# Chunked scan with a two-layer MLP: the first sweep's second matmul in plain fp32, decay masks moved ahead of the sums, and partial sums added by accumulating transfers

## The chip, the cores and the metric

The kernel runs on one core of a Trainium2 chip. TensorE (PE), VectorE (DVE), ScalarE (ACT), GpSimd (POOL) and SyncE (SP, which issues the transfers) each work through their own list of instructions in order, and wait for one another by semaphores. The metric is the device time of one execution in microseconds, the median over runs.

## The reference

Four batches of eight heads are scanned in chunks; the result, transposed to 3072 tokens of 256 values, goes through a two-layer MLP.

```python
cum = np.cumsum(log_a_chunk, axis=-1)
L = np.exp(cum[:, :, :, None] - cum[:, :, None, :]) * causal
M = np.einsum('bhin,bhjn->bhij', Cc, Bc) * L
y = np.einsum('bhij,bhjd->bhid', M, xc)
y += np.einsum('bhin,bhnd->bhid', Cc, state) * np.exp(cum)[:, :, :, None]
state = decay_full * state + np.sum(Bx, axis=2)

h = x @ w_in              # x: 3072 x 256, w_in: 256 x 2048
g = h - np.tanh(h)
out = g @ w_out           # w_out: 2048 x 256
```

The weights arrive as float64, all else is float32.

## The kernel before

**The scan.** The kernel cuts each batch of 768 positions into seven chunks of up to 112 (`Q`), 28 in all. A chunk needs the matrix `lt` (the decays, exponentials of differences of running sums, times C·B, zero above the diagonal), then `chunk_y` multiplies it by `x` on PE. The state that a chunk hands on stands in 16 extra rows of the next chunk's `x`, copied there by ACT (`copies`, L566), so that the chunks are a chain. The output of a chunk is split into two fp32r numbers, `xh` (ACT) and `xl` (DVE), so that two or three fast fp32r products give nearly a full fp32 product.

Chunks 0 to 2, which the first tile of tokens needs, get `lt` in `first_tile`: for each half of the heads, `fn_f` sums the logs `la` on PE into `cp`, `fn_x` takes four exponentials on ACT with a bias `ncum` for each head (L404), `fn_m` multiplies by C·B on DVE (L409), and `fn_s` zeroes what lies above the diagonal on POOL (L414). Chunks 3 to 9 get their sums from PE instead (`chunk_a`, L451), from tiles `lt_c` and `rt_c` of sums in three bf16 parts, which are sent through DRAM (`put_parts`, `get_parts`). `rt_c` is first filled with signs by `signs` on POOL (L806). Later chunks read their sums back from DRAM (`chunk_l`).

**The weights.** A block `u` of 256 hidden columns of both weights is loaded by `load_w`, and `conv` builds floats out of the float64 bits: `fn0` on ACT (L300), `fn1` to `fn4` on DVE (L305, L310, L313, L317), `hi` on ACT (L321) and `lo` on DVE (L324). The last two leave the fp32r pair `wh`, `wl`. Block 0 is converted in two halves (w_in, then w_out), each later block whole.

**The MLP.** Tokens lie in eight tiles `t`, four of 256 and four of 512. The first four are done in four sweeps over the hidden dimension (`SWEEPS`), of two blocks `u` each, so that the weights can arrive meanwhile; the last four go over all of it at once. A step (t, f) is `mm1` (L629: 12 matmuls of 256 columns, xh·wh + xh·wl + xl·wh), `act` (tanh on ACT, L643; the subtraction on DVE, L647; the split of `g` into `gh` on ACT, L651, and `gl` on DVE, L657) and, two steps later, `mm2` (L683: 12 matmuls again, into the PSUM bank `po0`). After the first sweep `keep` copies a tile's partial sum to SBUF (`pt`, L705); after the second and third DVE adds to it (L698), and after the last DVE adds (L717) and SP stores.

**What sets the order.** Nothing is written out by hand: `Order` collects every operation with a cost and its reads and writes, and a list scheduler with a seeded jitter (`SEED`, `JITTER`, `LOOK`, `RATE`, `URGE`) writes one list for each engine. A change of a cost or of a seed so moves rows everywhere. Tiles rotate through few buffers (`ph` 2, `g` 3, `att` 1).

Of the kernel before, what the change touches and what calls it, by code (L numbers as in the profile page):

```python
# [20 lines left out]
P = 128  # L21
# [5 lines left out]
Q = P - N  # L27
# [13 lines left out]

REBIAS = 2.0 ** -112
# [6 lines left out]
APART, URGE = 5, 3.0  # L49


class Order:
# [3 lines left out]
    DMA_LATENCY, SEM, SEM_PE, RATE, FLIGHT = 0.8, 0.15, 0.28, 0.24e6, 8  # L56
    ROUNDS, JITTER, SEED, EARLY, LOOK = 16, 0.3, 69, 5.0, 0.35
# [153 lines left out]
def tile_ssm_moe(ctx: ExitStack, tc: tile.TileContext, a, x, bn, bc, wts, out):  # L211
# [76 lines left out]
    wl = cp.tile([P, NCONV, 2, 2, 256], F32R, name="wl")  # L288

    def conv(u, halves=False):  # L290
# [36 lines left out]
        for i in range(n):  # L327
# [6 lines left out]
            op("DVE", 1.2 * k, lambda s=s: fn3(s), r=[n_v[i]], w=[n_m[i]])  # L334
            op("DVE", 1.2 * k, lambda s=s: fn4(s), r=[n_m[i]], w=[n_v[i]])
# [42 lines left out]
    def first_tile():  # L378
# [32 lines left out]

        def fn_s(ck, i):
            lt = chs[ck]["l"][:, 4 * i : 4 * i + 4]
            nc.gpsimd.affine_select(out=lt, in_=lt, pattern=[[0, 4], [1, Q]], compare_op=ALU.is_ge,  # L414
                                    fill=0.0, base=N, channel_multiplier=-1)

        for ck in range(len(chunks[0])):
# [4 lines left out]
            for i in range(2):  # L422
                n_f = slot("ph", NPH)
                op("PE", 1.2, lambda ck=ck, i=i: fn_f(ck, i), r=["la", "upto"], w=[n_f])
                op("ACT", 1.05, lambda ck=ck, i=i: fn_x(ck, i), r=[n_f, "ncum", "tab"], w=[k["n_l"][i]], urge=URGE)
# [80 lines left out]
    def chunk_y(ck):  # L506
# [68 lines left out]
        def copies(n):  # L575
            return [op("ACT", 0.2, lambda i=i: fn_c(i), r=[n], w=[grp[(ck + 1) // CPG]["p_x"][(ck + 1) % CPG]], urge=first) for i in range(4)]
# [4 lines left out]
        cost = 0.72 if far else 0.62 if apart else 0.81  # L581
# [52 lines left out]

    def act(t, f):
        n_h, n_g = gs[t, f, 0]
        n_gh, n_gl = slot("gh", 3), slot("gl", 3)
        gs[t, f, 0] += [n_gh, n_gl]
# [22 lines left out]
        op("DVE", 0.69, fn_s, r=[n_h], w=[n_g])  # L661
        op("ACT", 0.62, fn_h, r=[n_g], w=[n_gh])
        op("DVE", 0.71, fn_l, r=[n_g, n_gh], w=[n_gl])

    def mm2(t, f, seg):

        w, last = WIDTH[t], f + blocks(t) == seg[1]
        _, _, n_h, n_l = gs[t, f, 0]
# [19 lines left out]
        op("PE", 12 * rate(w) * blocks(t), fn, r=[n_h, n_l, f"wh{f // 2}.1", f"wl{f // 2}.1"], w=n_po[t, seg])  # L688
# [19 lines left out]

    def store(t, seg):
        w = WIDTH[t]  # L710
        name = op.pieces(slot("ob", 2), 2)

        def fn_c(e):
            if e == 0:
                obs[t] = p2.tile([P, 2, w], F32, tag="ob", name=f"ob{t}")
            if t < NSW:
                nc.vector.tensor_tensor(out=obs[t].rearrange("p e w -> p (e w)"), in0=po[t, seg][2], in1=pts[t], op=ALU.add)  # L717
            elif e == 0:
# [7 lines left out]
        if t < NSW:  # L726
            op("DVE", 0.69, lambda: fn_c(0), r=[*n_po[t, seg], n_pt[t]], w=name)
        else:
            for e in range(2):
                op(("ACT", "DVE")[e], 0.6, lambda e=e: fn_c(e), r=[n_po[t, seg][e]], w=[name[e]])  # L730
# [13 lines left out]
    ncf = cp.tile([P, N], F32, name="ncf")  # L744
    idn = cp.tile([P, N], F32, name="idn")
# [72 lines left out]
    op("POOL", 1.6, consts_pool, w=["upto", "after", "pid"])  # L818
    op("DVE", 0.25, logs, r=["al"], w=["a"])
# [4 lines left out]
    op("ACT", 0.9, ones, w=["lt_c"])  # L824

# [68 lines left out]
    conv(1)  # L894
# [91 lines left out]
```

## Time and profile before

| | |
|---|---|
| median of 3 runs | 337.64 us (335.47 to 447.55) |
| the profiled execution, its time | 337.02 us |
| its span, first to last instruction | 335.1 us |
| what lies around the span | 1.92 us |
| PE busy | 321.2 us (96%) |
| DVE busy | 226.3 us (68%) |
| ACT busy | 218.3 us (65%) |
| POOL busy | 57.0 us (17%) |

The run of 447.55 us stands alone; the other two and the profiled execution lie within 0.7% of one another. The shares are averages over stages that differ: the scan and the first sweep take the first 62 us, and the rest is nearly all matmuls. Busy time of PE is counted to modelled ends of pipelined matmuls, so that a step's length is better read from the start of one step to the start of the next.

### The profile page before, as it was taken

The numbers are of one execution on the slowest core, as the hardware profiler recorded it, in microseconds if no ns is written. First come the engines' busy times: TensorE is split into PE (matmuls) and PEld (weight loads), VectorE is DVE, ScalarE is ACT, GpSimd is POOL, SyncE is SP. The second block draws the span as 40 slices with busy tenths as digits, with TensorE's granted clock in tenths as the row PEclk, the third lists the DMA queues.
The fourth block names the chain that finished last, engine by engine and source line by source line (L and its number), as shares of the span: only waits on it lengthen the run. The fifth ranks groups of instructions, "written<-read, shape, count | busy, mean of one in ns | idle before, by whom it ended". The sixth has DMA issues, their size and how long they took to land.

```text
span 335.1 us, 6403 instructions
## 1 busy us (share of the span) xinstructions
PE 321.2 (96%) x2452; PEld 269.7 (80%) x2452; DVE 226.3 (68%) x346; ACT 218.3 (65%) x524; POOL 57.0 (17%) x77
## 2 busy tenths in 40 slices
PE   8867989899999999999999999999999999999995
PEld 7656878899999999877877777877787778888884
DVE  5898999999888855764556656456655554545552
ACT  7868889797666635856778783676676664544441
POOL 7445463121000200301111101121011010000000
PEclk9967999999999999999999999999999999999999
DMA  7759885280000006622432033323010000100001
GB/s 219 233 183 344 234 299 161 88 298 3 0 2 2 1 33 220 209 87 86 139 121 94 32 117 99 121 94 115 13 63 2 1 0 2 63 0 2 0 0 63
DMA packets 14441, 32.16 MB, mean 96 GB/s; under 512 B 2500, under 2 KB 5452, under 8 KB 14412
## 3 DMA queue, kind: packets, MB, share of 16 engines
q1 hardware_dynamic: 14412, 31.77, 28.4%
q8 instruction: 19, 0.31, 0.4%
q14 instruction: 10, 0.08, 0.1%
HBM read 28.33 MB, written 3.43 MB: 95 GB/s over the span
## 4 chain that ended last, share of the span: by engine, by line
PE 82%; DMA 8%; DVE 4%; ACT 2%; SPq 1%; issue 1%; POOL 0%; POOLq 0%
PE o L683 39%; PE ph L629 38%; DMA raw<-w_d 5%; PE y L541 3%; PE att L528 2%; DMA bc<-bc_d 2%; DMA braw<-bn_d 1%; ACT wv L300 1%; ACT lt L404 1%; DVE gl L657 1%; ACT x L566 0%; SPq L871 0%; DVE g L647 0%; DVE wm L305 0%; DVE xl L572 0%
## 5 line engine op out<-in xcount | busy, mean ns | idle before, releaser
L647 DVE TENSOR_TENSOR g<-ph,g 128x512 f32<-128x512 f32 x96 | 66.0, 689 | 67.6 <-ACT g L643 67.4
L643 ACT ACTIVATE g<-ph 128x512 f32<-128x512 f32 x96 | 57.2, 597 | 67.6 <-PE ph L629 65.9
L629 PE MATMUL ph<-xh,wh 128*128 128x256 f32 (+1 forms) x256 | 85.8, 346 | 0.0
L629 PE MATMUL ph<-xh,wl 128*128 128x256 f32 (+1 forms) x256 | 84.6, 341 | 0.0
L657 DVE TENSOR_TENSOR gl<-g,gh 128x512 fp32r<-128x512 f32 x96 | 68.8, 716 | 20.0 <-ACT gh L651 18.9
L651 ACT CAST gh<-g 128x512 fp32r<-128x512 f32 x96 | 59.5, 620 | 26.4 <-DVE g L647 25.4
L683 PE MATMUL o<-gh,wh 128*128 128x256 f32 (+1 forms) x256 | 72.2, 343 | 0.1
L683 PE MATMUL o<-gh,wl 128*128 128x256 f32 (+1 forms) x256 | 71.2, 339 | 0.0
L683 PE MATMUL o<-gl,wh 128*128 128x256 f32 (+1 forms) x256 | 70.8, 338 | 0.0
L629 PE MATMUL ph<-xl,wh 128*128 128x256 f32 (+1 forms) x256 | 65.8, 338 | 0.2 <-DVE xl L572 0.2
L476 POOL TENSOR_SCALAR_AFFINE_SELECT lt<-lt 128x896 f32<-128x896 f32 (+1 forms) x25 | 28.0, 1121 | 202.9 <-ACT lt L494 180.4
L629 PEld LDWEIGHTS ph<-xh,wh 128*128 128x128 f32 x256 | 49.2, 192 | 7.8 <-issue 1.6
L629 PEld LDWEIGHTS ph<-xh,wl 128*128 128x128 f32 x256 | 49.2, 192 | 5.3
L629 PEld LDWEIGHTS ph<-xl,wh 128*128 128x128 f32 x256 | 44.3, 191 | 6.0 <-DVE xl L572 0.4
L683 PEld LDWEIGHTS o<-gh,wh 128*128 128x128 f32 x256 | 41.5, 188 | 7.8 <-issue 1.9
L683 PEld LDWEIGHTS o<-gl,wh 128*128 128x128 f32 x256 | 41.6, 189 | 5.5
L683 PEld LDWEIGHTS o<-gh,wl 128*128 128x128 f32 x256 | 41.4, 188 | 5.2
L494 ACT ACTIVATE lt<-lt,ncum 128x112 f32<-128x112 f32 (+1 forms) x144 | 41.9, 377 | 0.0
L541 PE MATMUL y<-lt,x 128*32 128x128 f32 (+2 forms) x448 | 18.0, 275 | 6.4 <-ACT wh L321 3.1
L541 PEld LDWEIGHTS y<-lt,x 128*32 128x32 f32 x448 | 10.7, 110 | 14.0 <-issue 6.1
L532 DVE TENSOR_TENSOR lt<-att,lt 128x896 f32<-128x896 f32 (+1 forms) x18 | 19.0, 1058 | 0.0
L564 ACT COPY x<-s 16x64 f32<-16x64 f32 x60 | 14.4, 241 | 1.4 <-DVE s L559 0.7
(79 smaller groups left out, 229.8 us busy)
## 6 DMA issues: line engine op xcount, KB each, us to landing
lt<-cumr SPq DMA_DIRECT2D x18, 512.0 KB
raw<-w_d SPq DMA_DIRECT2D x16, 512.0 KB
bc<-bc_d SPq DMA_DIRECT2D x14, 352.0 KB
x<-x_d SPq DMA_DIRECT2D x14, 256.0 KB
out_d<-ob SPq DMA_DIRECT2D x8, 256.0 KB
braw<-bn_d SPq DMA_DIRECT2D x14, 112.0 KB
out_d<-ob SPq DMA_DIRECT2D x8, 128.0 KB
cum<-parts SPq DMA_DIRECT2D x1, 168.0 KB
```

The costliest lines, as they stand in the source:

```text
L476: nc.gpsimd.affine_select(out=k["l"][:, :, 0:q], in_=k["l"][:, :, 0:q], pattern=[[0, H], [1, q]], compare_op=ALU.is_ge, fill=0.0, base=N, ...
L494: nc.scalar.activation(k["l"][:, h, 0:q], k["l"][:, h, 0:q], AF.Exp, bias=ncum[:, h, ck : ck + 1])
L528: nc.tensor.matmul(out=a_[:, i], lhsT=bb[r], rhs=cc[r, :, 0 : qlen(ck + 1 + j)], start=True, stop=True)
L532: nc.vector.tensor_tensor(out=l, in0=chs[j]["a"], in1=l, op=ALU.mult)
L541: nc.tensor.matmul(out=y[r, hg * P : hg * P + P] if both else v[r, hg], lhsT=d["x"][:, cg, P * hg + D * h : P * hg + D * h + D], rhs=k["wh ...
L564: nc.scalar.copy(to.rearrange("p (g h d) -> p g h d", g=2, h=4)[:, :, i], k["s"][D * i : D * i + N])
L629: nc.tensor.matmul(out=ph[:, i * w : i * w + w], lhsT=w_[:, u, 0, k, j * P : (j + 1) * P], rhs=(xh, xl)[p][:, k, ts], start=p == 0 and k = ...
L643: nc.scalar.activation(g, gs[t, f][0], AF.Tanh)
L647: nc.vector.tensor_tensor(out=g, in0=ph, in1=g, op=ALU.subtract)
L651: nc.scalar.copy(gh, gs[t, f][1])
L657: nc.vector.tensor_tensor(out=gl, in0=g, in1=gh.bitcast(F32), op=ALU.subtract)
L683: nc.tensor.matmul(out=po[t, seg][e], lhsT=w_[:, u, 1, j, e * P : (e + 1) * P], rhs=g[:, i * w : i * w + w], start=f == seg[0] and k == 0 ...
```

## The change

Four things change, and with them the order everywhere.

- **The first sweep.** For tiles 0 to 3 and blocks 0 and 1 (`native`: 8 steps), `mm2` takes `g` and an unsplit weight `wf` as plain fp32: 4 matmuls of 256 columns in place of 12 fp32r ones. `gh` and `gl` are not made in these steps. `conv` leaves w_out of the two blocks in `wf`; its split is made by `parted` before tile 4 begins. Block 1 is now converted in halves, as block 0 was.
- **The masks of chunks 0 to 2.** POOL writes the logs into a 128x512 tile of `g`'s buffers with zeros where they don't count (`fn_k`), PE sums these, on top of a bf16 matmul that adds -32768 above the diagonal (`eye` by `never`), and ACT takes one exponential over four heads without a bias. `fn_s` is gone, and `ncum` is no longer waited for here.
- **The partial sums.** `add` copies the sum from PSUM on ACT to a buffer `ob`, and a transfer that POOL issues adds it to `pt` in SBUF. The last sweep's output is stored from `pt`.
- **The parts in DRAM** have another layout: two transfers put them there, eight fetch them (before: one and twelve). `signs` moves from POOL to DVE.

```diff
-    DMA_LATENCY, SEM, SEM_PE, RATE, FLIGHT = 0.8, 0.15, 0.28, 0.24e6, 8
-    ROUNDS, JITTER, SEED, EARLY, LOOK = 16, 0.3, 69, 5.0, 0.35
+    DMA_LATENCY, SEM, SEM_PE, RATE, FLIGHT = 0.8, 0.15, 0.28, 0.32e6, 8
+    ROUNDS, JITTER, SEED, EARLY, LOOK = 16, 0.3, 159, 5.0, 0.5
...
+            if whole(s):
+                op("DVE", 1.2 * k, lambda s=s: fn4(s), r=[n_m[i], n_v[i]], w=[f"wf{u}"])
+                continue
...
+    def parted(u, after):
+        w_ = wf[:, u].rearrange("p (k c) -> p k c", k=2)
+        op("ACT", 0.62, lambda: nc.scalar.copy(wh[:, u, 1], w_), r=[f"wf{u}"], w=[f"wh{u}.1"], after=after)
+        op("DVE", 0.7, lambda: nc.vector.tensor_tensor(out=wl[:, u, 1], in0=w_, in1=wh[:, u, 1].bitcast(F32), op=ALU.subtract),
+           r=[f"wf{u}", f"wh{u}.1"], w=[f"wl{u}.1"])
...
+        def fn_k(ck, i):
+            chs[ck]["k", i] = p3.tile([P, BANK], F32, tag="g", name=f"lm{ck}_{i}").rearrange("p (h m) -> p h m", h=4)
+            nc.gpsimd.affine_select(out=chs[ck]["k", i], in_=la[:, 4 * i : 4 * i + 4, ck : ck + 1].broadcast_to([P, 4, P]),
+                                    pattern=[[0, 4], [-1, P]], compare_op=ALU.is_gt, fill=0.0, base=0, channel_multiplier=1)
...
+            nc.tensor.matmul(out=f[:, :, 0:Q], lhsT=eye, rhs=never.unsqueeze(1).broadcast_to([P, 4, Q]),
+                             start=True, stop=False, skip_group_check=True)
             for h in range(4):
-                nc.tensor.matmul(out=f[:, h, 0:Q], lhsT=la[:, 4 * i + h, ck : ck + 1].broadcast_to([P, P]),
-                                 rhs=upto[:, N:P], start=True, stop=True)
+                nc.tensor.matmul(out=f[:, h, 0:Q], lhsT=chs[ck]["k", i][:, h], rhs=upto[:, N:P], start=False, stop=h == 3,
+                                 skip_group_check=True)
...
-            for h in range(4):
-                nc.scalar.activation(chs[ck]["l"][:, 4 * i + h, :], chs[ck]["f", i][:, h, 0:Q], AF.Exp,
-                                     bias=ncum[:, 4 * i + h, ck : ck + 1])
+            nc.scalar.activation(chs[ck]["l"][:, 4 * i : 4 * i + 4], chs[ck]["f", i][:, :, 0:Q], AF.Exp)
...
-        def fn_s(ck, i):
-            lt = chs[ck]["l"][:, 4 * i : 4 * i + 4]
-            nc.gpsimd.affine_select(out=lt, in_=lt, pattern=[[0, 4], [1, Q]], compare_op=ALU.is_ge,
-                                    fill=0.0, base=N, channel_multiplier=-1)
...
+    def native(t, f):
+        return t < NSW and f // 2 < WHOLE
...
+            if native(t, f):
+                for i in range(blocks(t)):
+                    for e in range(2):
+                        u, j = divmod(f + i, 2)
+                        nc.tensor.matmul(out=po[t, seg][e], lhsT=wf[:, u, 256 * j + e * P : 256 * j + (e + 1) * P],
+                                         rhs=gs[t, f][1][:, i * w : i * w + w], start=f == seg[0] and i == 0 and e == 0,
+                                         stop=last and i == blocks(t) - 1, skip_group_check=True)
+                return
...
-            op("DVE", 0.69, lambda: nc.vector.tensor_tensor(out=pts[t], in0=po[t, seg][2], in1=pts[t], op=ALU.add),
-               r=n_po[t, seg], w=[n_pt[t]])
+            add(t, seg)
...
+        op("ACT", 0.6, fn, r=n_po[t, seg], w=[name])
+        op("POOL", 1.0, lambda: nc.gpsimd.dma_start(out=pts[t], in_=obs[t], accum_op=ALU.add), r=[name], w=[n_pt[t]])
...
-        nc.gpsimd.tensor_scalar(out=v, in0=nc.const_aps.tensor(1.0, (P, 1), F32).broadcast_to(v.shape),
+        nc.vector.tensor_scalar(out=v, in0=nc.const_aps.tensor(1.0, (P, 1), F32).broadcast_to(v.shape),
...
-    conv(1)
+    conv(1, True)
...
+    for u in range(WHOLE):
+        plan(begin["t", NSW] - 6 + 2 * u, lambda u=u: parted(u, [len(op.ops) - 1]))
```

DVE's list at the start of the program, before (`a_sb` are the inputs a, `braw` takes constant rows, `both` the running sums out of PSUM):

```order
L797 COPY braw_94<-idn 16x256
L797 COPY braw_95<-idn 16x256
L797 COPY braw_96<-idn 16x256
L779 TENSOR_SCALAR a_sb<-a_sb 128x224
L876 TENSOR_SCALAR ncum<-pr 128x224
L850 COPY both<-pr 112x256
```

The same place on DVE in the changed kernel:

```order
L836 TENSOR_SCALAR a_sb<-a_sb 128x224
L863 TENSOR_SCALAR rt_c<-const-float32-1.0,par 128x896 x2
L854 COPY braw_97<-idn 16x256
L854 COPY braw_98<-idn 16x256
L854 COPY braw_99<-idn 16x256
L910 COPY both<-pr 112x256
```

The signs come in and the constant rows move behind the inputs' clamp; `ncum` leaves this place.

DVE's list from the second step of block 0's conversion to chunk 2's `lt`, before (`lt_173`, `lt_214` and `lt_274` are chunks 0, 1 and 2):

```order
L310 TENSOR_SCALAR wv_201<-wv_201 128x512
L313 SCALAR_TENSOR_TENSOR wm_192<-wv_201,wm_192 128x512
L317 SCALAR_TENSOR_TENSOR wv_201<-wv_201,wm_192 128x512
L409 TENSOR_TENSOR lt_214<-att_178,lt_214 128x4x112 x2
L572 TENSOR_TENSOR xl<-y_232,xh 128x2x112
L305 TENSOR_SCALAR wm_192<-raw_139 128x512
L310 TENSOR_SCALAR wv_201<-wv_201 128x512
L313 SCALAR_TENSOR_TENSOR wm_192<-wv_201,wm_192 128x512
L317 SCALAR_TENSOR_TENSOR wv_201<-wv_201,wm_192 128x512
L409 TENSOR_TENSOR lt_274<-att_178,lt_274 128x4x112
L324 TENSOR_TENSOR wl<-wv_201,wh 128x512
L409 TENSOR_TENSOR lt_274<-att_178,lt_274 128x4x112
```

The same place on DVE in the changed kernel (`lt_193`, `lt_234`, `lt_283`):

```order
L432 TENSOR_TENSOR lt_193<-att_207,lt_193 128x4x112 x2
L318 SCALAR_TENSOR_TENSOR wm_197<-wv_184,wm_197 128x512
L325 SCALAR_TENSOR_TENSOR wv_184<-wv_184,wm_197 128x512
L315 TENSOR_SCALAR wv_184<-wv_184 128x512
L432 TENSOR_TENSOR lt_234<-att_207,lt_234 128x4x112 x2
L588 TENSOR_TENSOR xl<-y_249,xh 128x2x112
L318 SCALAR_TENSOR_TENSOR wm_197<-wv_184,wm_197 128x512
L332 TENSOR_TENSOR wl<-wv_184,wh 128x512
L325 SCALAR_TENSOR_TENSOR wf<-wv_184,wm_197 128x512
L432 TENSOR_TENSOR lt_283<-att_207,lt_283 128x4x112 x2
```

The same instructions stand between chunk 0's and chunk 2's `lt` in another order; the second half's last step now writes `wf`.

POOL's list where the second sweep begins, before (`lt_752` and the like are chunks whose cut is made here):

```order
L497 TENSOR_TENSOR lt_752<-braw_96,wdec 128x8x16
L476 AFFINE_SELECT lt_752<-lt_752 128x8x112
L497 TENSOR_TENSOR lt_929<-braw_96,wdec 128x8x16
L476 AFFINE_SELECT lt_929<-lt_929 128x8x112
L357 COPY bc_1025<-idn 128x2x16
L497 TENSOR_TENSOR lt_1112<-braw_94,wdec 128x8x16
L476 AFFINE_SELECT lt_1112<-lt_1112 128x8x112
```

The same place on POOL in the changed kernel (`part_4_...` are partial sums of the second sweep):

```order
L513 TENSOR_TENSOR lt_822<-braw_99,wdec 128x8x16
L492 AFFINE_SELECT lt_822<-lt_822 128x8x112
L375 COPY bc_981<-idn 128x2x16
L753 DMA pt_556<-part_4_1032 128x512
L753 DMA pt_699<-part_4_1110 128x512
L513 TENSOR_TENSOR lt_1116<-braw_97,wdec 128x8x16
L753 DMA pt_841<-part_4_1206 128x512
L492 AFFINE_SELECT lt_1116<-lt_1116 128x8x112
```

Chunk cuts now stand behind transfers that wait for ACT's copy of a partial sum.

## Rows read from the trace of the kernel before

**Rows 1.** Windows by stage: busy time and count per engine, PE clock, DMA share, GB/s.

```profile
16.20:21.30 5.10, 2.03 (x31) 1.18 (x29) 5.03 (x9) 3.36 (x11) 1.82 (x3) 0.72 0.27 55
18.50:28.70 10.20, 8.95 (x94) 7.19 (x95) 9.62 (x13) 6.22 (x15) 4.80 (x6) 0.50 0.83 274
28.70:62.00 33.30, 28.09 (x433) 24.40 (x432) 32.13 (x41) 27.90 (x64) 16.11 (x15) 1.00 0.73 242
62.00:331.30 269.30, 269.30 (x1771) 226.12 (x1768) 169.93 (x259) 168.87 (x403) 25.14 (x38) 1.00 0.19 63
331.30:335.10 3.80, 0.00 (x1) 0.00 (x0) 0.69 (x1) 0.00 (x0) 0.00 (x0) 1.00 0.36 138
```

**Rows 2.** Waits of PE from 28.7 to 62 us: total, times, longest.

```profile
PE att L451 <- DVE lt L464: 1.5, 2, 1.1
PE y L541 <- DVE xl L572: 1.5, 1, 1.5
PE y L541 <- issue: 1.3, 1, 1.3
```

**Rows 3.** Groups of DVE from 28.7 to 62 us, costliest first: busy, mean ns.

```profile
L657 DVE TENSOR_TENSOR gl<-g,gh 128x512 fp32r<-128x512 f32 x7 | 6.3, 896 | 0.1
L464 DVE TENSOR_TENSOR lt<-att,lt 128x896 f32<-128x896 f32 (+1 forms) x5 | 5.3, 1055 | 0.2 <-ACT lt L460 0.2
```

**Rows 4.** Timeline of the start, several engines: start, duration, engine, line; idle before.

```profile
2.13 4.56 POOL L806 TENSOR_SCALAR rt_c<-const-float32-1.0,par 128x784 bf16<-128x784 f32 x2
2.23 1.36 DVE L797 COPY braw<-idn 16x256 f32<-16x256 f32 x3
3.51 0.26 DVE L779 TENSOR_SCALAR a_sb<-a_sb 128x224 f32<-128x224 f32 x1
...
5.19 0.54 PE L845 MATMUL pr<-la,upto 128*128 128x224 f32 x2
5.57 1.93 PE L387 MATMUL cp<-upto,la 128*128 128x112 f32 x16
5.77 0.39 DVE L876 TENSOR_SCALAR ncum<-pr 128x224 f32<-128x224 f32 x1 [2.00 <-PE pr L845]
6.08 0.41 DVE L850 COPY both<-pr 112x256 f32<-112x256 f32 x1
...
9.34 0.43 DVE L305 TENSOR_SCALAR wm<-raw 128x512 uint32<-128x512 uint32 x1 [1.26 <-DMA raw<-w_d]
```

**Rows 5.** The timeline further on, from 12 to 27 us.

```profile
12.13 0.88 SPq L865 DMA_DIRECT2D lt_c<-cum  x1
...
18.11 0.62 DVE L409 TENSOR_TENSOR lt<-att,lt 128x448 f32<-128x448 f32 x1
18.16 0.76 SPq L868 DMA_DIRECT2D rt_c<-cum  x2
...
18.80 0.58 POOL L414 TENSOR_SCALAR_AFFINE_SELECT lt<-lt 128x448 f32<-128x448 f32 x1 [0.16 <-DVE lt L409]
...
19.25 0.60 PEld L541 LDWEIGHTS y<-lt,x 128*32 128x32 f32 x16 [3.16 <-POOL lt L414]
...
20.19 0.38 PE L451 MATMUL att<-rt_c,lt_c 9*128 9x224 bf16 x4
...
21.30 0.58 PE L629 MATMUL ph<-xh,wh 128*128 128x256 f32 x1
...
26.55 0.58 PE L629 MATMUL ph<-xh,wh 128*128 128x256 f32 x1
```

**Rows 6.** The chain that ended last, merged: start, duration.

```profile
63.59 1.42 PE o L683 x12
...
78.68 0.57 PE y L541 x16
```

**Rows 7.** POOL's cut of that chunk's matrix, timeline.

```profile
69.42 1.23 POOL L476 TENSOR_SCALAR_AFFINE_SELECT lt<-lt 128x896 f32<-128x896 f32 x1 [9.46 <-ACT lt L494]
```

More of the change, by code (lines that the diff above doesn't have):

```diff
@@ L288, in tile_ssm_moe @@
     wl = cp.tile([P, NCONV, 2, 2, 256], F32R, name="wl")
+    wf = cp.tile([P, WHOLE, 512], F32, name="wf")
     def conv(u, halves=False):
@@ L295, in part, with whole @@
             return v[:, s].bitcast(F32)
+        def whole(s):
+            return u < WHOLE and s.start == 1
         def fn0(s):
@@ L450, in fn_p @@
                 r = slice(32 * i, 32 * i + 9)
-                nc.tensor.matmul(out=at_[:, i, 0:2, :], lhsT=lt_c[r, ck - NEAR.start], rhs=rt_c[r, :, ck - NEAR.start, 0:q],
+                nc.tensor.matmul(out=at_[:, i, 0:2, :], lhsT=lt_c[r, ck - NEAR.start], rhs=rt_c[r, :, ck - NEAR.start, N : N + q],
                                  start=True, stop=True)
@@ L575, in copies @@
         def copies(n):
-            return [op("ACT", 0.2, lambda i=i: fn_c(i), r=[n], w=[grp[(ck + 1) // CPG]["p_x"][(ck + 1) % CPG]], urge=first) for i in range(4)]
+            return [op("ACT", 0.2, lambda i=i: fn_c(i), r=[n], w=[grp[(ck + 1) // CPG]["p_x"][(ck + 1) % CPG]],
+                       urge=first) for i in range(4)]
         first = URGE if ck < len(chunks[0]) else 0.0
         r, w = [*k["n_l"], d["p_x"][cg], *([] if far or apart else [d["n_bw"]])], [n_y]
-        cost = 0.72 if far else 0.62 if apart else 0.81
+        cost = 0.72 if far else 0.62 if apart else 0.85
         if apart:
@@ L661, in act @@
         op("DVE", 0.69, fn_s, r=[n_h], w=[n_g])
+        if native(t, f):
+            return
         op("ACT", 0.62, fn_h, r=[n_g], w=[n_gh])
@@ L707, in keep, with add, fn @@
         op("ACT", 0.6, fn, r=n_po[t, seg], w=[n_pt[t]])
+    def add(t, seg):
+        name = slot("ob", 2)
+        def fn():
+            obs[t] = p2.tile([P, BANK], F32, tag="ob", name=f"part{t}_{seg[0]}")
+            nc.scalar.copy(obs[t], po[t, seg][2])
+        op("ACT", 0.6, fn, r=n_po[t, seg], w=[name])
+        op("POOL", 1.0, lambda: nc.gpsimd.dma_start(out=pts[t], in_=obs[t], accum_op=ALU.add), r=[name], w=[n_pt[t]])
     def store(t, seg):
         w = WIDTH[t]
+        if t < NSW:
+            add(t, seg)
+            for e in range(2):
+                op("SP", 0.42, lambda e=e: nc.sync.dma_start(out=out[e * P : (e + 1) * P, START[t] : START[t] + w],
+                                                             in_=pts[t][:, e * w : e * w + w]), r=[n_pt[t]], dma=KB * w // 256)
+            return
         name = op.pieces(slot("ob", 2), 2)
@@ L724, in fn_d @@
             nc.sync.dma_start(out=out[e * P : (e + 1) * P, START[t] : START[t] + w], in_=obs[t][:, e])
[L726 to L730, printed above, removed]
+        for e in range(2):
+            op(("ACT", "DVE")[e], 0.6, lambda e=e: fn_c(e), r=[n_po[t, seg][e]], w=[name[e]])
         for e in range(2):
@@ L744, in tile_ssm_moe @@
     ncf = cp.tile([P, N], F32, name="ncf")
+    eye = cp.tile([P, P], BF16, name="eye")
+    never = cp.tile([P, Q], BF16, name="never")
     idn = cp.tile([P, N], F32, name="idn")
@@ L818, in tile_ssm_moe @@
     op("POOL", 1.6, consts_pool, w=["upto", "after", "pid"])
+    op("POOL", 1.0, masks, w=["never"])
     op("DVE", 0.25, logs, r=["al"], w=["a"])
@@ L824, in tile_ssm_moe @@
     op("ACT", 0.9, ones, w=["lt_c"])
+    for w in range(2):
+        op("DVE", 0.85, lambda w=w: signs(w), r=["par"], w=["rt_c"])
     for G in range(2):
@@ L875, in tile_ssm_moe @@
     op("PE", 0.34, lambda: sums_cols(upto, "pq"), r=["la", "upto"], w=[n_pr])
-    first = op("DVE", 0.33, lambda: nc.vector.tensor_scalar(out=ncum.rearrange("p h c -> p (h c)"), in0=misc["pq"][:, 0:NHC],
+    op("DVE", 0.33, lambda: nc.vector.tensor_scalar(out=ncum.rearrange("p h c -> p (h c)"), in0=misc["pq"][:, 0:NHC],
                                                     scalar1=-1.0, scalar2=None, op0=ALU.mult), r=[n_pr], w=["ncum"])
-    op("DVE", 0.36, lambda: split(0), r=[n_pr], w=["rows"], after=[first])
+    op("DVE", 0.36, lambda: split(0), r=[n_pr], w=["rows"])
     op("DVE", 1.4, lambda: [split(i) for i in range(1, 6) if i != 4], r=["rows"], w=["parts"])
-    op("SP", 0.42, put_parts, r=["parts"], w=["cum3"], dma=KB)
+    for i in range(2):
+        op("SP", 0.42, lambda i=i: put_parts(i), r=["parts"], w=["cum3"], dma=KB)
     for i in range(2):
```

64 lines of the change are left out of this document (38 added, 26 removed).

## Prediction

> **What bounds the kernel now.** I read the windows by stage first. From 62 to 331.3 us PE is busy for 269.3 of 269.3 us while DVE and ACT stand at 63%: nothing there pays but PE work, more or less of it [rows 1]. After the last matmul come 3.8 us of copies and stores, which the change leaves alone [rows 1]. What can be won lies before 62 us, in three places.
>
> First, a hole. From 16.2 to 21.3 us PE is busy for 2.03 of 5.1 us [rows 1]. The timeline shows why: chunk 2's product y waits 3.16 us for its matrix, which DVE finishes at 18.73 and POOL then cuts for 0.58 us; y starts at 19.25, and the first MLP step at 21.30 [rows 5].
>
> Second, the clock. From 18.5 to 28.7 us PE is granted half of its clock (1.2 of 2.4 GHz), just behind that hole, and is busy for 8.95 us of it [rows 1]. At the full clock this work would take half: 4.5 us are lost.
>
> Third, DVE. From 28.7 to 62 us DVE is busy for 32.13 of 33.3 us and PE for 28.09, so 5.2 us of PE are idle [rows 1]. The waits name DVE for 3.0 us of it, and 1.3 us have no releaser [rows 2]. The costliest group of DVE there is `gl`, 6.3 us for seven [rows 3].
>
> So 3.07 + 4.5 + 5.2 us, 12.8 in all, is the most that a better start could give back, and each part has its own gate.
>
> **The change part by part**, against the profiled execution: 335.1 us of span and 1.92 around it, 337.02 in all, 0.6 below the median shown.
>
> *Plain fp32 in `mm2`.* A step now takes 1.42 us [rows 6]. The new one has 4 fp32 matmuls of 256 columns. No fp32 matmul of 256 columns stands in the trace; the nearest show that the hardware makes two records of each instruction. One with 224 columns starts at 5.19 and is followed at 5.57, so 0.19 us for a record and 0.217 for one of 256 columns; 8 records make 1.74 us. The 112-column ones take 1.93 us for 16 records, 0.12 each [rows 4], which scaled by columns is 0.276, or 2.2 us for a step. In the shorter ones the weight load can be what limits, and behind 256 columns it has more room, so I stay near the lower end, with a little for the change of weights: 1.80 us. The surplus is 0.38 x 8 = +3.0 us (2.6 to 6.3), and it is on the path, since these steps lie where PE becomes the bound. The Trainium skill, page "Perfetto Trace Analysis", section "Engine Utilization", gives PE's output rate as halved for the low-high form of fp32; by it an estimate is 1.71 us for a step and +2.3 us for eight, a little below my lower end.
>
> *The mask as a matmul.* Six bf16 matmuls of 448 columns are new. A twelfth of today's step, a record of 256 columns, is 0.118 us [rows 6], so 448 are 0.21, and six are 1.2 us. I cost them at nothing: they lie ahead of chunk 2's y, where PE waits 3.16 us anyway [rows 5]. If that cover went, they would cost the 1.2.
>
> *Chunk 2's y.* Three things leave its chain (four short exponentials become one long one, the bias, the cut), but DVE's list decides. Between `both` and chunk 2's second product the two kernels hold the same DVE instructions in another order (the two passages of the list in the change). Before, DVE ran from 5.77 to 18.73 with 1.3 us of waiting for weights in it, so 11.6 us of work [rows 4, 5]. After, it starts later: the signs come behind `a_sb`, which ends at 3.77, and the constant rows, 1.36 us, behind these [rows 4]. DVE's signs have no row; 512 elements of another tensor-scalar take 0.43 us [rows 4], so 896 take 0.75, and a two-input operation on 896 takes 1.06 [rows 3]; I take 0.9, 1.8 for both, where POOL took 4.56 [rows 4]. The list then starts at 3.77 + 1.8 + 1.36 = 6.9 and ends near 18.5 if it never waits, at 18.2 if the signs take 0.75 each. With no cut behind it y starts at 18.2 to 18.6, not at 19.25.
>
> Behind y in PE's list stands chunk 3's sum, which needs the parts by way of DRAM. SP fetched them from 12.13 to 18.92 and the matmul came at 20.19 [rows 5]. Now the parts are ready 0.9 us later (6.9 against 6.08 for `both`), and there are 8 fetches. If each takes what one of the `lt_c` fetches took, 0.7 to 0.9, they end at 18.6 to 20: no earlier. So the first MLP step comes at 20.2 to 21.3, and I put the gain at -0.7 us (0 to -1.2).
>
> *The clock.* PE still has a hole of about two microseconds before chunk 2's y and another before chunk 3's sum, with little work between. The clock fell 2.3 us into such a hole, and I expect it to fall again. It should come back sooner, because the second MLP step (26.55 today [rows 5]) no longer waits for all of block 1: its w_in half is converted alone, so PE runs with fewer holes in between. I take 2.0 of the 4.5 us back (0 to -4.5).
>
> *DVE from 28.7 to 62.* The eight `gl` leave, and the splits of two w_out halves; some 6.3 us of 32.1 go [rows 3], so DVE has 26 us of work there and PE 28.1 + 3.0. PE is then the bound, and most of its 5.2 us of idle should go; the chain from chunk to chunk, ACT's small copies and POOL's cuts stay. I take 3.5 (1.5 to 5.2). What is late next there is PE itself.
>
> *The rest.* Twelve DVE additions leave and twelve ACT copies come, in the sweeps where ACT is 63% busy [rows 1]: nothing. The splits in `parted`, two instructions on ACT and two on DVE over 512 elements, none longer than the 0.9 us of a `gl` [rows 3], come after 62 us, where both have room: nothing. An accumulating transfer has no row. It must end before the tile's next one, a sweep away: 16 steps of 1.42 us or more [rows 6], 22 us. What stands behind it is dealt with below. On SP the stores from `pt` now stand behind tile 4's, and nothing waits for them.
>
> The sum: 3.0 - 0.7 - 2.0 - 3.5 = -3.2, so 337.02 - 3.2 = **333.8 us**.
>
> **The rivals.**
>
> *The clock holds.* If chunk 2's y comes sooner than I think (signs at 0.75 us or less, a list without the slow spells of today's), the hole is shorter and the other 2.5 us come back: 331.3. With all the idle gone too (another 1.7) and the native surplus at 2.6, it is 329.2. For it: the fall comes behind one hole only, and the clock is full in every other window after it [rows 1]. Against: the new order leaves the hole where it was.
>
> *Plain fp32 is dear.* If a record is bound by its weights as in the 112-column rows, a step is 2.2 us and the surplus 6.3 [rows 4]. With the start no better (0 for y and the clock) and 3.5 us from DVE the sum is +2.8: 339.8, slower than before. It decides from 2.2 us for a step on, where 8 x 0.78 exceeds what the start returns; at the forecast's other terms it is 337.1. Against it: the 224-column record at 0.19.
>
> *The start does not change.* DVE's late start uses up what the cut gave, and y, chunk 3 and the clock stand as they were: 337.0 + 3.0 - 3.5 = 336.5.
>
> *GpSimd's transfers hold its queue.* In the second sweep chunk cuts stand in POOL's list behind transfers (the third passage). Today a cut ends at 70.65, and the y that needs it starts at 78.68, 8 us later [rows 6, 7]. In the new order nine MLP steps of 1.42 us, 12.7 us, lie on PE between the partial sum that feeds `pt_841` and the y behind the next cut; less 0.9 for ACT's copy, as for a `gl` of the same size [rows 3], and 1.2 for the cut [rows 7], a transfer may hold POOL for 10.6 us. From there on each further microsecond stops PE at each of the four cuts that stand behind transfers; at 14 us it is 4 x 3.4 = +13.6, 347. Against it: 14 us are more than any row of POOL shows for such a tile. The Trainium skill, page "SBUF — State Buffer", section "Who interferes with whom", says that a DMA issued by GpSimd can be starved while DVE holds the port pair that the two share; this is a way to such a hold, and no run here shows it yet.
>
> **How the numbers follow.** The forecast (332 to 336) has 0.48. The clock alone holding (331.3) has 0.13, with the idle gone as well (329.2) 0.13; dear fp32 (337.1 to 339.8) 0.10; the unchanged start 0.08; the held queue 0.08. Two per cent, 6.7 us, is about what a measurement of this kernel can tell from no change: below 330.9 is faster, above 344.4 slower. The best case and a third of the one before it lie below 330.9: 0.18. The held queue alone lies above: 0.08. The rest is 0.74. The range leaves out the held queue, half of the best case and the edge of dear fp32: 329.5 to 339.5.
>
> **What would show it.** A native step takes 1.75 to 1.9 us on PE. Chunk 2's y starts between 18 and 18.7 us, chunk 3's sum near 20, and the granted clock falls near 18 us but is back before 27. From 28 to 60 us DVE is below 85% busy, and PE's idle there is under 2.5 us. The prediction is wrong if the clock never falls, if a native step takes over 2 us, if PE waits for POOL after 62 us, or if the parts land so late that the first MLP step starts after 22 us.

## The result and the profile after

The changed kernel takes 332.06 us (median of 4 runs, 331.81 to 332.45), the kernel before beside it 337.45 (median of 3, 335.47 to 337.64; a fourth execution of 447.55 us stands alone, its cause isn't known, and it is left out). The ratio, made from the runs themselves and not from the medians, is 0.985, with a 95% interval of 0.982 to 0.989: a gain of 1.2 to 1.8%. The prediction said 333.8, within 329.5 to 339.5. The profiled execution of the changed kernel took 332.45 us, 330.8 of it span; before it was 337.02 and 335.1. The span lost 4.3 us.

The windows by stage of the changed kernel answer to [rows 1] (busy time and count on PE, PEld, DVE, ACT, POOL; granted clock, DMA share, GB/s):

```profile
16.20:21.30 5.10, 2.72 (x94) 2.14 (x86) 4.55 (x10) 3.49 (x13) 0.98 (x2) 0.87 0.56 160
18.50:28.70 10.20, 8.88 (x144) 7.43 (x145) 7.92 (x14) 7.39 (x21) 3.69 (x5) 0.83 0.96 317
28.70:62.00 33.30, 32.72 (x396) 27.57 (x395) 29.67 (x39) 27.32 (x67) 11.92 (x14) 1.00 0.64 228
62.00:327.00 265.00, 264.65 (x1724) 219.66 (x1722) 161.83 (x244) 169.65 (x399) 36.17 (x48) 1.00 0.26 76
327.00:330.80 3.80, 0.00 (x0) 0.00 (x0) 0.38 (x1) 0.00 (x0) 0.00 (x0) 0.97 0.37 138
```

After 62 us PE has 264.65 us of work left, where it had 269.3: 4.65 us less, and up to its last matmul (at 326.65) it is never idle there in either kernel. So the whole gain was made before 62 us. Behind the last matmul the changed kernel takes 4.1 us and not 3.8; with DVE's additions in place of the transfers (e2 below) it is 3.8 again. From 28.7 to 62 us PE's idle time went from 5.2 to 0.6 us; the granted clock from 18.5 to 28.7 us rose from 0.50 to 0.83; the early hole is shorter by 0.7 us.

PE's waits over the whole span (total, times, longest) answer to [rows 2]:

```profile
PE y L557 <- ACT x L582: 1.9, 1, 1.9
PE att L467 <- DVE lt L480: 0.8, 1, 0.8
PE y L557 <- issue: 0.5, 2, 0.3
PE z L569 <- ACT x L582: 0.5, 1, 0.5
```

The 3.0 us for DVE between 28.7 and 62 are gone, and no wait names POOL. DVE's costliest groups from 28.7 to 62 us, as in [rows 3], show that `gl` left (its first stands at 63.0) and that conversions lead the list with `lt`; DVE is busy for 29.67 us in place of 32.13, so other work has moved into most of what `gl` freed:

```profile
L480 DVE TENSOR_TENSOR lt<-att,lt 128x896 f32<-128x896 f32 (+1 forms) x5 | 5.3, 1055 | 0.9 <-ACT lt L476 0.9
L318 DVE SCALAR_TENSOR_TENSOR wm<-wv,wm 128x1024 uint32<-128x1024 uint32 (+1 forms) x4 | 4.7, 1186 | 0.0
L670 DVE TENSOR_TENSOR g<-ph,g 128x512 f32<-128x512 f32 x7 | 4.7, 684 | 0.9 <-ACT g L666 0.9
```

The timeline of the start, beside [rows 4]: both signs take DVE 1.27 us together, where POOL took 4.56, and `both` comes at 6.60 (before 6.08).

```profile
3.49 1.27 DVE L863 TENSOR_SCALAR rt_c<-const-float32-1.0,par 128x896 bf16<-128x896 f32 x2
4.28 2.25 POOL L404 TENSOR_SCALAR_AFFINE_SELECT lm<-la 128x512 f32<-128x512 f32 x3 [1.08 <-ACT la L878]
4.68 1.99 DVE L854 COPY braw<-idn 16x256 f32<-16x256 f32 x3
6.60 0.40 DVE L910 COPY both<-pr 112x256 f32<-112x256 f32 x1
```

The timeline from 12 to 25 us, beside [rows 5]: the last part is fetched at 16.79 and not after 18; chunk 2's matrix is ready at 18.17 and its y starts at 18.57 (before 19.25), behind `xl` of the chunk before (18.10 and 0.37 long), whose PSUM buffer (`po1` has one) it takes over; the ACT copy that the row names ended at 17.76; chunk 3's sum comes at 19.21, the first MLP step at 20.71, the second at 24.12 (before 20.19, 21.30 and 26.55).

```profile
16.79 0.44 SPq L926 DMA_DIRECT2D rt_c<-cum  x1
17.03 1.14 DVE L432 TENSOR_TENSOR lt<-att,lt 128x448 f32<-128x448 f32 x2
18.10 0.37 DVE L588 TENSOR_TENSOR xl<-y,xh 128x224 fp32r<-128x224 f32 x1
18.57 0.59 PE L557 MATMUL y<-lt,x 128*32 128x112 f32 x16 [1.90 <-ACT x L582]
19.21 0.28 PE L467 MATMUL att<-rt_c,lt_c 9*128 9x224 bf16 x4
20.71 0.58 PE L646 MATMUL ph<-xh,wh 128*128 128x256 f32 x1
24.12 0.39 PE L646 MATMUL ph<-xh,wh 128*128 128x256 f32 x1
```

The chain that ended last, merged, with native steps behind a chunk's work, two of them in a row, and one between first matmuls (`mm1`):

```profile
27.89 1.93 PE o L706 x8
38.32 1.92 PE o L706 x8
48.89 3.65 PE o L706 x16
61.04 1.73 PE o L706 x8
```

The second of two in a row adds 1.72 us, so a record takes 0.215 to 0.216 us, and 0.2 us come on top where the step follows a chunk's y. A split step pays that too: between first matmuls it takes the 1.42 us of [rows 6], and behind a chunk's y, in the kernel before:

```profile
79.26 1.61 PE o L683 x12
```

Like for like, a native step costs 0.31 to 0.32 us more than a split one.

And the accumulating transfers (first the group of line 753, then the time to landing; below it a cut with a transfer behind it, beside [rows 7]):

```profile
L753 POOL DMA_DIRECT2D pt<-part x12: 859/870/1169, 69.3 to 135.8; - x12
...
DMA to landing us min/median/max: 3.3/3.3/5.4
```

```profile
98.28 1.72 POOL L492 TENSOR_SCALAR_AFFINE_SELECT lt<-lt 128x768 f32<-128x768 f32 x1 [3.73 <-ACT lt L510]
99.94 0.87 POOL L753 DMA_DIRECT2D pt<-part  x1
```

### The profile page after: what moved, and what is told of

It is laid out like the page before. It is cut to its first block, busy times and chain, and to the rows that moved or that the text cites. A ratio compares the mean times of both kernels' runs of the same rounds, so it can differ in the third digit from the quotient of the medians.

```text
span 330.8 us, 6359 instructions
## 1 busy us (share of the span) xinstructions
PE 322.1 (97%) x2426; PEld 267.6 (81%) x2426; DVE 216.0 (65%) x333; ACT 216.7 (66%) x512; POOL 61.7 (19%) x91
## 4 chain that ended last, share of the span: by engine, by line
PE 94%; ACT 2%; DVE 2%; issue 1%; ACTq 0%
PE ph L646 40%; PE o L716 38%; PE y L557 4%; PE o L706 4%; PE att L544 3%; PE cp L412 2%; PE warm L871 1%; DVE lt L480 1%; ACT x L582 1%; ACT lt L476 1%; PE att L472 0%; PE cp L409 0%; DVE wv L315 0%; PE att L422 0%; ACT wv L305 0%
## 5 line engine op out<-in xcount | busy, mean ns | idle before, releaser
L680 DVE TENSOR_TENSOR gl<-g,gh 128x512 fp32r<-128x512 f32 x88 | 61.5, 700 | 25.2 <-ACT gh L674 23.1
L674 ACT CAST gh<-g 128x512 fp32r<-128x512 f32 x88 | 54.5, 620 | 28.9 <-DVE g L670 27.7
L716 PE MATMUL o<-gh,wh 128*128 128x512 f32 (+1 forms) x224 | 67.3, 352 | 0.0
L716 PE MATMUL o<-gl,wh 128*128 128x512 f32 (+1 forms) x224 | 65.6, 345 | 0.0
L716 PE MATMUL o<-gh,wl 128*128 128x512 f32 (+1 forms) x224 | 65.6, 345 | 0.0
L492 POOL TENSOR_SCALAR_AFFINE_SELECT lt<-lt 128x896 f32<-128x896 f32 (+1 forms) x25 | 27.3, 1091 | 144.6 <-ACT lt L510 132.3
L716 PEld LDWEIGHTS o<-gh,wh 128*128 128x128 f32 x224 | 36.9, 188 | 8.2 <-issue 2.2
L716 PEld LDWEIGHTS o<-gl,wh 128*128 128x128 f32 x224 | 36.9, 188 | 5.9
L716 PEld LDWEIGHTS o<-gh,wl 128*128 128x128 f32 x224 | 36.9, 188 | 5.3
L557 PE MATMUL y<-lt,x 128*32 128x128 f32 (+2 forms) x448 | 17.1, 270 | 2.4 <-ACT x L582 1.9
L753 POOL DMA_DIRECT2D pt<-part x12 | 10.9, 906 | 45.4 <-ACT part L750 45.4
L557 PEld LDWEIGHTS y<-lt,x 128*32 128x32 f32 x448 | 10.2, 109 | 10.0 <-issue 6.9
(90 smaller groups left out, 269.3 us busy)
```

Source lines behind the costliest of these rows:

```text
L492: nc.gpsimd.affine_select(out=k["l"][:, :, 0:q], in_=k["l"][:, :, 0:q], pattern=[[0, H], [1, q]], compare_op=ALU.is_ge, fill=0.0, base=N, ...
L557: nc.tensor.matmul(out=y[r, hg * P : hg * P + P] if both else v[r, hg], lhsT=d["x"][:, cg, P * hg + D * h : P * hg + D * h + D], rhs=k["wh ...
L674: nc.scalar.copy(gh, gs[t, f][1])
L680: nc.vector.tensor_tensor(out=gl, in0=g, in1=gh.bitcast(F32), op=ALU.subtract)
L716: nc.tensor.matmul(out=po[t, seg][e], lhsT=w_[:, u, 1, j, e * P : (e + 1) * P], rhs=g[:, i * w : i * w + w], start=f == seg[0] and k == 0 ...
L753: op("POOL", 1.0, lambda: nc.gpsimd.dma_start(out=pts[t], in_=obs[t], accum_op=ALU.add), r=[name], w=[n_pt[t]])
```

## The experiments

Two sums from windows of 1 us go with each run, both for 4 to 62 us of the profiled execution: PE's idle time, and the clock loss (half of what PE was busy at half clock). Before they are 9.3 and 4.5 us, after 3.7 and 1.5. Ratios are against the kernel before, with 95% intervals; in these runs its median was 336.6 to 336.9.

The theory was this: the plain fp32 steps free DVE, so that PE becomes the bound before 62 us and their surplus is paid in full; the masks bring y forward and the clock back; the transfers cost nothing. The rival was the order: RATE, SEED and LOOK are in the diff too, and every list was made anew.

**One part undone at a time**, with the new numbers; each edit also makes the planner lay out all lists again.

Without plain fp32 (e1):

```diff
 def native(t, f):
-    return t < NSW and f // 2 < WHOLE
+    return False
...
```

> The changed kernel with the first sweep's second matmul as 12 fp32r matmuls again (wf, native and parted unused); all else as changed, the order planned anew. Theory (the plain fp32 steps cost PE 0.5 us each and pay by taking DVE off the path): PE work falls by 8 x 0.51 = 4.1 us, but the eight gl and two splits return to DVE, which is again busy over 93% from 28.7 to 62 us, and 3 to 5 us of PE idle come back there: 332 to 334 us. Rival (the plain steps are only a cost, the gain is from the masks and the order): PE idle stays under 1.5 us and the time is 328 to 329 us.

Measured: 337.28 us, ratio 1.001 (0.998 to 1.003). The whole gain is gone; idle 7.0 us, clock loss 5.8. Windows of this kernel:

```profile
18.50:28.70 10.20, 8.93 (x112) 6.94 (x109) 9.41 (x15) 5.51 (x13) 3.17 (x4) 0.67 0.93 313
28.70:62.00 33.30, 29.19 (x404) 25.00 (x396) 30.42 (x39) 27.70 (x66) 14.60 (x14) 0.90 0.70 230
```

PE's idle from 28.7 to 62 us, 4.1 us, is what the theory had said (3 to 5); DVE is busy for 91% there, a little under its 93. The time misses both ranges: on top of these holes the clock is low twice (0.67 from 18.5 to 28.7 us, and 0.90 from 28.7 to 62, where before and after both have 1.00). The order is another one too, and other orders of the changed kernel (below) lose 2.6 to 4.6 us with plain fp32 in place, so what of the 5.2 us is plain fp32 isn't separated.

With the masks as before (e3: the bias in four exponentials, POOL's cut, no mask matmul):

```diff
-op("POOL", 0.7, lambda ck=ck, i=i: fn_k(ck, i), r=["la"], w=[n_k], urge=URGE)
...
+op("POOL", 0.8, lambda ck=ck, i=i: fn_s(ck, i), w=[k["n_l"][i]], urge=URGE)
```

> The changed kernel with chunks 0 to 2 as before: four exponentials with a bias for each half, POOL's cut behind DVE's product, no mask matmuls. Theory: chunk 2's y starts 0.5 to 1.5 us later, the hole ahead of it is longer, and the low clock lasts longer than the 3.4 us of the changed kernel: 333.5 to 336 us. Rival (the masks are beside the point, DVE's list sets y): within 0.7 of 332 us.

Measured: 335.92 us, 0.995 (0.992 to 0.998); idle 5.8, clock loss 3.1. The time lies in the theory's range, but not by its mechanism. Chunk 2's y does start 1.35 us later, at 19.92, yet PE waits only 0.89 us just ahead of it and the clock stays full there; it falls at 26.0 us, with the second MLP step at 33.04 (24.12 in the changed kernel). Block 1's weights are issued late in this order, which the section on the order takes up.

With DVE's additions in place of copy and transfer (e2):

```diff
-            add(t, seg)
+            op("DVE", 0.69, lambda: nc.vector.tensor_tensor(out=pts[t], in0=po[t, seg][2], in1=pts[t], op=ALU.add),
+               r=n_po[t, seg], w=[n_pt[t]])
```

> The changed kernel with the partial sums added by DVE from PSUM into pt, without ACT's copy and without the accumulating transfers. Theory: after 62 us only PE work counts, DVE and ACT have a third of their time free, so 332 us within 0.8. Rival (the transfers carry a part of the gain, or cost something): 334 us or more, or 330 us or less.

Measured: 333.91 us, 0.989 (0.985 to 0.994); idle 4.8, clock loss 1.7. That is outside the theory's 0.8, just short of the rival's 334. But the 1.9 us against the changed kernel are lost before 62 us, ahead of the first transfer at 69.3: from 62 to 322 us PE is busy for 260.00 of 260 us in both. So the transfers as such gain and cost nothing there; what differs is the order of the start.

**Is PE the bound before 62 us?** Half of the native work taken out (e6: the second hidden block of 128 columns is left out of the product in the eight native steps; no other list changes):

```diff
 for i in range(blocks(t)):
-    for e in range(2):
+    for e in range(2 if i == 0 else 0):
...
-        stop=last and i == blocks(t) - 1, skip_group_check=True)
+        stop=last and i == 0, skip_group_check=True)
```

> The changed kernel, its order unchanged, with 2 in place of 4 plain fp32 matmuls in each of the 8 steps: the second of the two hidden blocks of 128 columns is left out of the sum there. It takes 8 x 0.96 = 7.7 us of PE work out of the first sweep. Theory (PE is now the bound of that sweep): the time falls by 5 us or more, to 324 to 327 us. Rival (DVE, ACT or the chain of chunks bounds it): by less than 3.5 us, to 328.5 us or more.

Measured: 331.72 us, 0.984 (0.979 to 0.989). Eight steps lost four records of 0.216 us each, 6.9 us of PE work (the expectation's 7.7 is too much), and the time fell by 0.3; PE's idle time from 4 to 62 us rose from 3.7 to 10.5. One window and the two longest waits of PE in 30 to 62 us:

```profile
28.70:62.00 33.30, 27.45 (x369) 22.68 (x362) 29.95 (x39) 27.47 (x67) 11.50 (x14) 1.00 0.68 230
```

```profile
PE y L557 <- POOL lt L492: 1.7, 1, 1.7
PE y L557 <- issue: 1.4, 1, 1.4
```

The 5.3 us that PE no longer works there it stands idle. This part of the theory falls: in this order the first sweep runs at the pace of its chunks, and the native steps fill time in which PE would wait. From 28.7 to 62 us its waits name DVE for 2.6 us, POOL for 1.7 and nothing for 1.4. In the profiled execution the clock stayed full to the last matmul; the other three executions had a mean granted clock of 0.988 to 0.995, so whether it falls at the start differs between executions of one kernel.

**The order.** The changed kernel with the old RATE, SEED and LOOK (e4), with the old RATE alone (e13), with other seeds (e10, e11), and the kernel before with the new numbers (e5) or another seed (e12):

```diff
 e4:  RATE 0.32e6 -> 0.24e6, SEED 159 -> 69, LOOK 0.5 -> 0.35
 e13: RATE 0.32e6 -> 0.24e6
 e10: SEED 159 -> 69          e11: SEED 159 -> 160
 e5 (before):  RATE 0.24e6 -> 0.32e6, SEED 69 -> 159, LOOK 0.35 -> 0.5
 e12 (before): SEED 69 -> 160
```

> The changed kernel with the planner's old numbers (RATE 0.24e6, SEED 69, LOOK 0.35). Theory (the operations carry the gain): 331.5 to 334.5 us. Rival (the order that the new numbers happen to give carries it): 335.5 us or more.

> The kernel before with the planner's new numbers alone (RATE 0.32e6, SEED 159, LOOK 0.5). Theory (the operations carry the gain): 335.5 to 340 us. Rival (the numbers carry it): 334 us or less.

> The changed kernel with SEED 69 in place of 159, RATE and LOOK as changed. Theory (the operations give room in the first 62 us, and the order decides how much of it is used): anywhere from 331 to 337 us, with the difference to the changed kernel in PE's idle and half-clock time before 40 us and none after 62 us. Rival (the operations give the gain under any seed, RATE and LOOK took it away in the run with the old numbers): 331.5 to 333 us.

> The changed kernel with SEED 160, RATE and LOOK as changed. Theory and rival as for the run with SEED 69: 331 to 337 us by the theory, 331.5 to 333 by the rival. If both seeds lie above 334.5, the changed kernel's seed is a lucky one.

> The kernel before with SEED 160 alone. Theory (its operations leave DVE and the chain of chunks full until 62 us, so that no order gets far below): 335 to 340 us. Rival (the order alone can give what the change gave): 333.5 us or less.

> The changed kernel with RATE 0.24e6 alone in place of 0.32e6. Theory (the assumed transfer rate only reshuffles the order, as a seed does): 331 to 337 us. Rival (with the low rate the planner issues block 1's weights late, which costs the second MLP step and a second fall of the clock): 335.5 us or more, with the clock low for 6 us or more and the first load of block 1 issued after 15 us.

| kernel | median us | ratio (95%) | idle, clock loss us |
|---|---|---|---|
| changed | 332.06 | 0.985 (0.982 to 0.989) | 3.7, 1.5 |
| e11 changed, SEED 160 | 334.69 | 0.995 (0.993 to 0.997) | 4.9, 1.6 |
| e10 changed, SEED 69 | 335.28 | 0.998 (0.996 to 0.999) | 4.9, 1.7 |
| e13 changed, old RATE | 336.49 | 0.997 (0.994 to 1.000) | 5.5, 4.2 |
| e4 changed, old numbers | 336.67 | 1.000 (0.998 to 1.002) | 4.7, 4.9 |
| e5 before, new numbers | 336.84 | 0.999 (0.997 to 1.001) | 7.8, 4.9 |
| e12 before, SEED 160 | 337.82 | 1.002 (1.000 to 1.005) | 9.2, 5.9 |

The rival held for a large part: the same operations in another order give back from 2.6 us (another seed) to all of the gain (the old numbers). The numbers alone, without the operations, give nothing. Both seeds lie above 334.5, so by what was said ahead of e11 the changed kernel's seed is a lucky one. In e4 the place is seen: block 1's first load (the third `raw` in SP's list) is issued at 18.51 us, in the changed kernel at 9.83; in e13 at 18.24. From the timeline of SP in e4, and its windows of 2 us:

```profile
18.51 0.43 SPq L282 DMA_DIRECT2D raw<-w_d  x1
```

```profile
24.00:26.00 2.00, 0.70 (x32) 0.45 (x32) 1.05 (x2) 1.93 (x7) 0.00 (x0) 1.00 1.03 370
26.00:28.00 2.00, 1.87 (x40) 1.30 (x44) 1.97 (x5) 1.57 (x6) 1.45 (x2) 0.60 1.04 343
28.00:30.00 2.00, 1.57 (x15) 0.99 (x8) 1.97 (x4) 1.95 (x5) 0.00 (x0) 0.50 1.04 384
```

With no second block to work on PE is busy for 0.70 of 2 us from 24 to 26, and the clock falls a second time, from 26.4 to 33.2. In the changed kernel the second MLP step runs there.

The assumed rate isn't the cause by itself: with the new RATE that load is late in e10, e11 and e3 too (SP's timelines, in this order):

```profile
16.44 0.37 SPq L282 DMA_DIRECT2D raw<-w_d  x1
17.69 0.44 SPq L282 DMA_DIRECT2D raw<-w_d  x1
18.85 0.43 SPq L282 DMA_DIRECT2D raw<-w_d  x1
```

In all five orders with the load behind 16 us the second MLP step starts at 27.3 to 34.0 us, the clock falls near 26, and the time is 334.7 to 336.7; with the load near 10 us (the changed kernel, e6 and e8 with its order, and e2) the step starts at 23.0 to 24.1, the clock doesn't fall there, and the time is 331.3 to 333.9. That points at this load, but no run moves it alone, and e1, without plain fp32, is slow with the load at 4.57. It also means that e3 tells little of the masks.

**The clock.** PE kept busy with products that nothing reads, ahead of chunk 2's y: 8 in the changed kernel (e8), 13 in the kernel before (e9):

```diff
+if ck == 2:
+    busy = ps_h.tile([P, 4, P], F32, tag="ph", name="busy")
+    for i in range(8):
+        nc.tensor.matmul(out=busy[:, i % 4], lhsT=upto, rhs=upto, start=True, stop=True)
```

> The changed kernel with 8 matmuls of 128 columns that nobody reads (1.7 us at full clock) on PE between chunk 1's state and chunk 2's y, where PE stands idle for 1.9 us; the order is unchanged. Theory (the clock falls because of that hole, and its low stretch costs up to 1.5 us): the clock stays full near 20 us, or falls for a shorter stretch, and the time is 330.4 to 331.4 us. Rival (the low stretch is covered by other waits, or the clock falls anyway): 331.8 to 332.6 us.

> The kernel before with 13 matmuls of 128 columns that nobody reads (2.8 us at full clock) on PE between chunk 1's state and chunk 2's y, where it stands idle for 3.1 us; the order is unchanged. Theory (the 10 us at half clock come from that hole and cost up to 4.5 us): the clock stays full at 18.5 us and the time is 333 to 335 us. Rival (DVE and the transfers are what is late there, the clock costs little): 336 us or more even with a full clock.

Measured, e8: 331.30 us, 0.985 (0.982 to 0.988). That is 0.8 us below the changed kernel in the medians, but only 0.2 us in the ratios, and the intervals overlap. Timeline and windows of e8:

```profile
16.68 2.05 PE L556 MATMUL busy<-upto 128*128 128x128 f32 x16
18.66 0.59 PE L561 MATMUL y<-lt,x 128*32 128x112 f32 x16
```

```profile
16.20:21.30 5.10, 4.62 (x113) 3.99 (x106) 4.26 (x9) 3.46 (x13) 1.74 (x2) 1.00 0.65 182
18.50:28.70 10.20, 8.99 (x159) 7.09 (x161) 8.70 (x14) 7.75 (x21) 4.96 (x6) 1.00 1.00 334
```

The clock stays full, as the theory had it, and y stands where it was, now behind these products. That the time falls by it isn't shown clear of the noise.

Measured, e9: 337.93 us, 1.002 (0.999 to 1.005). The clock holds behind the hole at 18 us but falls behind later ones, near 27 and near 34 us (clock loss 3.4, idle 6.5). Windows of e9:

```profile
18.50:28.70 10.20, 8.05 (x114) 6.37 (x116) 10.00 (x13) 6.54 (x17) 5.17 (x6) 0.92 0.81 253
28.70:62.00 33.30, 29.06 (x412) 25.27 (x404) 31.30 (x39) 26.94 (x62) 15.97 (x15) 0.92 0.75 246
```

DVE is busy for 10.00 of 10.2 us and then 31.30 of 33.3: the kernel before is late by DVE, and a faster PE mostly waits more.

How much the clock is worth can be read from the executions as well, since each has its mean granted clock. Two of e9's ten kept the full clock (1.00) and took 335.32 and 335.39 us, the other eight, at 0.985 to 0.995, 336.41 to 339.58. The kernel before ran 69 times beside e1 to e13: 33 executions had the 0.985 of its profile and took 336.87 us on average, the eight with 0.994 or 0.995 took 336.05, the nine with 0.977 to 0.980 took 338.62. From 0.985 to 0.995 PE gets back some 3 us of its work, and the time falls by 0.8. The changed kernel, at 0.994 to 0.995, takes 331.81 to 332.45: some 4 us of the gain aren't the clock.

## Why the prediction came out right

The time fell 1.7 us under the forecast and inside its likeliest case. By its own terms, on the profiled execution (-4.3 us of span where -3.2 was said):

- *Native fp32, +3.0 (2.6 to 6.3).* The mechanism was right, the size a little high. A record takes 0.215 to 0.216 us, as scaled from the 224-column row (0.217); the change of weights costs 0.2 us behind a chunk's y, but a split step pays it there too. Like for like it is 8 x 0.31 = +2.5, just under the lower bound. The Trainium skill, "Perfetto Trace Analysis", "Engine Utilization", gave an estimate of 1.71 for the step; eight records make 1.73, so the trace agrees.
- *On the path.* This reason fell. "They lie where PE becomes the bound" is contradicted by e6: 6.9 us less of this work saved 0.3. The surplus filled idle time, and PE's busy 32.72 of 33.3 us is not the sign of a bound that I would have taken it for.
- *Chunk 2's y and the first MLP step, -0.7 (0 to -1.2).* Right: y at 18.57 in the 18.2 to 18.6 that were said, the step at 20.71 within 20.2 to 21.3, 0.6 us earlier. The parts landed earlier than I held possible (last fetch issued at 16.79), and what y waits for last is not its matrix but the PSUM buffer that `xl` at 18.10 gives back.
- *The clock, -2.0 (0 to -4.5).* It came back before 27, as said, but fell at 20.0 and not near 18; the low stretch ran from 20.0 to 23.4 us. PE lost 1.5 us of work by it in place of 4.5. The reason, the second MLP step being earlier, fits e4, where block 1 is late and the clock falls twice. The price was wrong: the forecast counts each microsecond of PE's work as one of time, and between executions of the kernel before, 3 us of such work were worth 0.8 us.
- *DVE from 28.7 to 62, -3.5 (1.5 to 5.2).* PE's idle time there fell by 4.6 us, to 0.6 (said: under 2.5). That DVE would be busy for less than 85% was wrong: it is 28.37 of 32 us from 28 to 60, 89%. Conversions moved into the room.
- *Masks at nothing.* The six mask matmuls lie ahead of chunk 2's y, which still waits 1.9 us: covered. What the new masks gain isn't settled: e3 loses most where block 1 is late, and another seed alone gives 335.28.
- *The transfers.* The rival of the held queue is ruled out: an issue holds POOL for 0.86 to 1.17 us, against the 10.6 from which it would count, and no PE wait names POOL. The starving of which the Trainium skill tells ("SBUF — State Buffer", "Who interferes with whom") is not seen at these twelve.

What the terms come to: idle -5.25 us in the whole span (13.95 to 8.7), PE busy +0.95. The second is native +2.5, clock -3.0, the masks about +1.2 by their terms in the forecast, less 0.5 for the six halves of the logs' sums beside them; that leaves some 0.75 that I can't place. This is a sum of PE's time, which says where it went and not what each part is worth.

What the prediction missed is that its largest uncertain quantity was the order and not a price. It kept the numbers of the planner out of its sum; with seed 69 or 160 the same operations would have given 334.7 to 335.3, and with the old numbers no change at all. That the time came out this low is in part the luck of the seed, and the sum met it with a term on the path that wasn't (native) and a clock priced too high.

The 2.6 to 3.2 us between seeds are medians, idle time and clock loss those of one execution. The profiled executions themselves differ by 1.5 us (e11, 333.97 against 332.45) and 2.4 (e10, 334.82), of which idle time and clock loss are 1.3 and 1.4.

Open: whether block 1's load alone makes the difference between the orders; what plain fp32 and the masks gain each in one and the same order; whether an order exists that brings the kernel before to 334, since only three were run; and what of e2's 1.9 us is the additions on DVE.

## What to carry to other kernels

An engine that is 98% busy in a stretch is not thereby the bound: take work off it and see whether the end moves. Where a planner with a seed sets the order, its scatter (here 3 us of 332) belongs into the range, and an edit's worth is known only against several orders of both versions. Compare a step's price like for like: one that follows other work (1.93 us) with one that does so too (1.61), not with one in a dense run (1.42). Time at half clock is PE's work lost, not time lost: where the chain beside PE was late, 3 us of it were worth 0.8, and filling the hole (e8, e9) gave nothing clear of the noise.

## What the runs showed of the hardware

- A transfer of 256 KB that adds into SBUF, issued by POOL, held POOL for 0.87 us (median) and landed 3.3 us after its issue (longest 5.4).
- A plain fp32 matmul of 256 columns leaves two records, 0.215 to 0.216 us each at full clock; four of them take 1.73 us between first matmuls and 1.93 behind a chunk's y, the split step of twelve 1.42 and 1.61.
- DVE wrote both sign tiles in 1.27 us; POOL took 4.56 us for slightly smaller ones (784 columns against 896).
- The mean granted clock differs between executions of one kernel, and the time with it: the kernel before had 0.977 to 0.995 and took 335.65 to 339.66 us beside e1 to e13; e9 had 0.985 to 1.00 and took 335.32 to 339.58.
